# Other first rounds of attention, later rank products, low parts and row sums on TensorE in three slots, and held loads before the last stage

## The chip, the cores and the metric

The kernel runs on one core of a Trainium2 chip. Its five engines have instruction queues of their own: TensorE (PE; its weight loads are listed apart as PEld), VectorE (DVE), ScalarE (ACT), GpSimd (POOL) and SyncE (SP). SyncE does no arithmetic here: it issues transfers between the memory of the chip (DRAM) and the on-chip memory, and every transfer runs on the same 16 DMA engines, whoever issues it. The metric is the device time of one launch in microseconds.

## The reference

Three parts follow one another, all in float32:

```
scores = q @ k^T / 8 - log(448)            # 4 batches, 12 heads, 448 tokens, 64 wide
x  = (1 / (1 + exp(-scores))) @ v          # to (1792 tokens, 768)
logits = norm(x) @ norm(emb)^T / tau       # 8 experts, each token takes the largest
y  = softmax(logits)[e] * (relu(x @ w1[e]) @ w2[e])    # 768 -> 1024 -> 768
h  = y @ w_in                              # 768 -> 2048
g  = (a0 + a1 h + a2 h^2 + a3 h^3) / (1 + |b0| |h| + |b1| h^2 + 1e-6)
out = g @ w_out                            # 2048 -> 768
```

## The kernel before

Most products are made at float32 accuracy from a high and a low part: an operand is rounded to a short float32 form (`fp32r`), the rest is kept as a second such number, and three products are summed (high with high, high with low, low with high).

**Attention** (`attention`) goes over 12 double pairs of heads, called rounds `T`. In a round TensorE makes the scores of two pairs (`scores`, three chunks of 128 keys each; the last 64 keys of both pairs share one tile, `scores3`), ScalarE takes the sigmoid, TensorE multiplies the pair of the round before with v (`values`, `values3`) and transposes it (`transp`), and VectorE copies it out. `load` issues a pair's four key and query transfers, `load_v` those of v for a group of three pairs. The program order within a round is the order on every engine's queue. Beside it, in steps (`work`), VectorE decodes blocks of the 64-bit last-stage weights (`side_work`, `decode_steps`), for which `fetch` issues raw blocks of 768 KB on SyncE. Its route (`route_steps`, a generator of which 11 steps are taken per round) picks the expert of each token; its rank product (L298 to L314) counts, on TensorE, how many tokens before a token chose the same expert. Ahead of the first scores TensorE runs 21 products of zeros (L361) as fillers.

**Experts** (`experts`). `plan` deals the tokens into at most 21 slots of one expert each. Slots 14 to 20 are run under a condition, and each slot exists in two forms of which one is taken by a branch: a full one (128 tokens) and a small one (up to 64 tokens, whose high and low parts share one set of columns). VectorE prepares each expert's weights in four half-weights, high (L671) and low (L678), and signals `rdy`; it waits for `don` from ScalarE before it overwrites a weight. In a slot the hidden rows are transposed (in the small form folded, L756) into PSUM, ScalarE copies them out as high part and as raw, and GpSimd subtracts them to the low part (L761, L768). In the small form the two halves of the result rows are copied out by ScalarE and added by GpSimd (L815). GpSimd also issues the gather of the token rows (L706) and their scatter (L858). `less` makes a low part on TensorE: it subtracts the high part from what already lies in PSUM, by a product with the negative identity, and ScalarE copies the rest out.

**Last stage** (`ffn`). Weight blocks are loaded (`load`), split into high and low (`split`, ScalarE and VectorE) and written back to DRAM (`keep`) for the three later token groups. `rows` loads 512 token rows, in four parts for the first group, `gate` scales them on VectorE, `first_x` runs 26 fillers, transposes the rows with 24 transposes and lets ScalarE and VectorE split them. Then `l1` and `l2` (L1004 to L1008 and L1052 to L1054) fill TensorE until the end.

Of the kernel before, what the change touches and what calls it, by code (L numbers as in the profile page):

```python
# [20 lines left out]
P = 128  # L21
# [10 lines left out]
NSLOT = 21  # L32
NSURE = 14
NPAIR = H // 2
NDP = B * NPAIR // 2
# [33 lines left out]
def constants(tc, st):  # L69
    nc = tc.nc  # L70
    cst = st["cst"]
    ident = cst.tile([P, P], F32, name="ident")
    nc.gpsimd.memset(ident, 0.0)
    nc.gpsimd.affine_select(
        out=ident, in_=ident, pattern=[[-1, P]], compare_op=ALU.not_equal, fill=1.0, base=0, channel_multiplier=1
    )
    iden = st["iden"]
    nc.gpsimd.tensor_copy(iden[:, :, :P], ident.unsqueeze(1).broadcast_to([P, NPAIR, P]))
    st["ident"] = ident
    neg = st["neg"] = cst.tile([P, P], F32R, name="neg")  # L80
    nc.gpsimd.tensor_scalar(neg, ident, -1.0, None, op0=ALU.mult)
    fold = st["fold"] = cst.tile([P, P // 2], F32, name="fold")
    nc.gpsimd.tensor_add(fold, ident[:, 0::2], ident[:, 1::2])
    bias_s = cst.tile([P, 1], F32, name="bias_s")
    nc.gpsimd.memset(bias_s, -math.log(S))
    st["bias_s"] = bias_s
# [39 lines left out]
def attention(tc, st, qT, kT, v, emb, tau, w_in, w_out, pa, pb):  # L126
# [16 lines left out]
    with ExitStack() as ctx:  # L143
# [8 lines left out]
        def load(pi):  # L152
            b, p = divmod(pi, NPAIR)
            qr = ap.tile([P, S], F32, name="qr", bufs=4)
            kr = ap.tile([P, S], F32, name="kr", bufs=4)
            for r in range(2):
                nc.sync.dma_start(kr[r * D : r * D + D], kT[b, :, 2 * p + r, :S])
                nc.sync.dma_start(qr[r * D : r * D + D], qT[b, :, 2 * p + r, :])
            pair[pi] = dict(q=qr, k=kr)
# [71 lines left out]

        def transp(pi):
            b, p = divmod(pi, NPAIR)
# [3 lines left out]
            for g in range(2):  # L237
                pt = pav.tile([P, 2, PW], F32, name="po", tag="po")
                for c in range(2):
                    c0 = (2 * g + c) * CP  # L240
                    nc.tensor.matmul(pt[:CP, c], lhsT=xs[:, c0 : c0 + CP], rhs=st["iden"][:, p], start=True, stop=True)  # L241
                nc.vector.tensor_copy(xrt[b][:CP, 2 * g : 2 * g + 2, p], pt[:CP])  # L242
# [15 lines left out]
        def route_steps(b):  # L258
# [25 lines left out]
            if not tail:  # L284
# [5 lines left out]
                else:  # L290
                    nc.vector.tensor_copy(OHs[:CP, b], s4)
            yield
            yield
# [62 lines left out]
        nc.gpsimd.dma_start(tr, tau.partition_broadcast(NE))  # L356
        load_v(0, 0, 2)
        load_v(0, 2, 4)
        load_v(1)
        wp = pav.tile([P, 512], F32, name="po")  # L360
        for _ in range(21):  # L361
            nc.tensor.matmul(wp, lhsT=wz[:, :P], rhs=wz, start=True, stop=True)
# [74 lines left out]
        for T in range(NDP + 2):  # L437
            if T < NDP:
                scores(2 * T)
            if T == 0:  # L440
                router_weights()
                load(2)
                load(3)
                for n in range(3):
# [9 lines left out]
            if T < NDP:  # L454
                work(2)
                scores(2 * T + 1)
            if T == 0:
                scores3(0)
            if 1 <= T <= NDP:
                transp(2 * T - 2)  # L460
                transp(2 * T - 1)
            if T + 2 < NDP:
                load(2 * T + 4)
                load(2 * T + 5)
            if T + 1 < NDP:
                scores3(T + 1)
# [168 lines left out]
def experts(tc, st, w1, w2, w_in, w_out):  # L635
# [5 lines left out]
    with ExitStack() as ctx:  # L641
# [106 lines left out]
        def h_hi(s, b0):  # L748
            d = S_[s]
            bb = slice(b0, b0 + 4)  # L750
            if d["small"]:
# [8 lines left out]
                nc.scalar.activation(raw, pt[:, :, :n], AF.Relu)  # L760
                nc.gpsimd.tensor_sub(lo, raw, hi)  # L761
                return
            pt = turn(d["hs"], b0, 4)
            hi, lo = full(d["h"], bb, 0), full(d["h"], bb, 1)
            nc.scalar.copy(hi, pt)
            raw = mp.tile([P, 4, P], F32, name="raw")
            nc.scalar.copy(raw, pt)
            nc.gpsimd.tensor_sub(lo, raw, hi)  # L768

        def h_lo(s, b0):  # L770
            pass

# [30 lines left out]
        def rows_out(s, u):  # L803
# [5 lines left out]
            if d["small"]:  # L809
                n = P // 2  # L810
                yl = mp.tile([n, N2], F32, name="yl", bufs=1)
                nc.scalar.copy(yl, py[n:])
# [99 lines left out]
def ffn(tc, st, out):  # L912
# [9 lines left out]
    with ExitStack() as ctx:  # L922
# [3 lines left out]
        ppa = ctx.enter_context(tc.tile_pool(name="fpa", bufs=1, space=PSUM, reuse_waits="tile"))  # L926
        X, R, WI, WO, G, acc, KEPT = {}, {}, {}, {}, {}, {}, {}

        def load(i):
# [29 lines left out]
        def rows(q, parts):  # L959
# [4 lines left out]
            for c in range(0, w // P, n):  # L964
                nc.sync.dma_start(yq[:, c : c + n], src[:, c : c + n])
            X[q] = dict(y=yq, n=w, c=w // P)
# [18 lines left out]
        def first_x():  # L985
            d = X[0]
            d["h"], d["l"] = [fw.tile([P, KD, 512], F32R, name=n) for n in ("xh", "xl")]
            pts = [ppa.tile([P, 512], F32, name=f"acc{k}") for k in range(KD)]
            for _ in range(26):
                nc.tensor.matmul(pts[0], lhsT=st["ones"], rhs=st["wz"], start=True, stop=True)  # L990
            for c in range(4):
                for k in range(KD):
                    nc.tensor.transpose(pts[k][:, c * P : (c + 1) * P], d["y"][:, c, k * P : (k + 1) * P], ident)  # L993
# [68 lines left out]

        for i in range(4):
            load(i)
        split(0)
        split(1)
        rows(0, 4)
        keep(0)
        load(4)
        load(5)  # L1070
        for c in range(4):
            gate(0, c)
        first_x()
        for i in range(NU + LF):
# [62 lines left out]
```

## Time and profile before

| | |
|---|---|
| median of three runs | 1045.91 us (1044.01 to 1048.17) |
| the profiled execution | 1043.8 us, its span 1042.0 us |
| TensorE busy | 1006.0 us, 97% of the span |
| VectorE, ScalarE, GpSimd busy | 722.6, 507.1, 143.6 us |
| mean granted clock of TensorE | 0.984 |
| attention, experts, last stage | to about 185, to about 550, to 1042 us |

A row of the timeline gives start, duration, engine, line, operation, output from inputs, form and count; in brackets stands the idle time before it and what ended that. [...] Matmul ends are modelled, so the spacing of starts says more than a duration.

### The profile page before, as it was taken

How to read it: one execution, taken by the hardware profiler on the slowest of the kernel's cores; microseconds unless marked ns; L12 is line 12 of the kernel's file. 1: busy time of each engine (PE TensorE's matmuls, PEld its weight loads, DVE VectorE, ACT ScalarE, POOL GpSimd, SP SyncE). 2: the span in 40 equal slices, each digit the busy share in tenths (PEclk: the TensorE clock that was granted, in tenths of full speed). 3: DMA queues.
4: the chain of work that ended last, by engine and by line, in shares of the span. 5: the costliest groups of instructions: out<-in, count | busy, mean ns of one | idle time of the engine just before them, and what ended most of it. 6: DMA issues, size and time to landing. Idle time of an engine off the chain costs nothing. (4 is left out here: it accounts for less than half of the span.)

```text
span 1042.0 us, 14389 instructions
## 1 busy us (share of the span) xinstructions
PE 1006.0 (97%) x5256; PEld 794.5 (76%) x5256; DVE 722.6 (69%) x1031; ACT 507.1 (49%) x860; POOL 143.6 (14%) x141
## 2 busy tenths in 40 slices
PE   8999999798999999999996999999999999999998
PEld 3444444487899898898984888888888888888998
DVE  1545564899706897296994999966766667666676
ACT  4557565632232332333333776745455564445664
POOL 2000000153323342242451000000000000000000
PEclk8999999899999999999998999999999999999999
DMA  7977886686915869267878986677655576555892
GB/s 215 273 226 208 230 256 205 208 279 220 348 50 180 260 204 370 86 221 286 270 218 326 418 333 262 267 251 293 219 182 181 188 273 208 195 194 193 323 400 88
DMA packets 106668, 250.22 MB, mean 240 GB/s; under 512 B 11912, under 2 KB 63240, under 8 KB 106576
## 3 DMA queue, kind: packets, MB, share of 16 engines
q1 hardware_dynamic: 103504, 234.40, 65.7%
q0 software_dynamic: 3072, 14.58, 4.1%
q8 instruction: 59, 0.97, 0.4%
q14 instruction: 33, 0.27, 0.1%
HBM read 193.89 MB, written 55.06 MB: 239 GB/s over the span
## 5 line engine op out<-in xcount | busy, mean ns | idle before, releaser
L1052 PE MATMUL acc<-gh,wo 128*128 128x512 f32 (+1 forms) x384 | 139.3, 363 | 0.3 <-DVE gh L1038 0.3
L1054 PE MATMUL acc<-gl,wo 128*128 128x512 f32 (+1 forms) x384 | 139.4, 363 | 0.0
L1053 PE MATMUL acc<-gh,wo 128*128 128x512 f32 (+1 forms) x384 | 139.2, 363 | 0.0
L1004 PE MATMUL ph<-xh,wi 128*128 128x512 f32 (+1 forms) x384 | 137.8, 368 | 0.1
L1005 PE MATMUL ph<-xh,wi 128*128 128x512 f32 (+1 forms) x384 | 136.1, 363 | 0.0
L1016 ACT COPY h<-ph 128x512 f32<-128x512 f32 (+1 forms) x64 | 34.1, 533 | 158.0 <-PE ph L1008 158.0
L1023 DVE SCALAR_TENSOR_TENSOR sq<-sq,ab,ab 128x512 f32<-128x512 f32 (+1 forms) x64 | 43.8, 684 | 90.6 <-ACT ab L1020 90.5
L1008 PE MATMUL ph<-xl,wi 128*128 128x512 f32 (+1 forms) x384 | 87.2, 363 | 0.0
L1004 PEld LDWEIGHTS ph<-xh,wi 128*128 128x128 f32 x384 | 72.5, 189 | 12.0 <-ACT xh L995 1.3
L1052 PEld LDWEIGHTS acc<-gh,wo 128*128 128x128 f32 x384 | 72.5, 189 | 11.8 <-DVE gh L1038 0.6
L1054 PEld LDWEIGHTS acc<-gl,wo 128*128 128x128 f32 x384 | 72.5, 189 | 11.4 <-DVE gl L1039 0.2
L1053 PEld LDWEIGHTS acc<-gh,wo 128*128 128x128 f32 x384 | 72.5, 189 | 11.1
L1005 PEld LDWEIGHTS ph<-xh,wi 128*128 128x128 f32 x384 | 72.6, 189 | 10.7
L1008 PEld LDWEIGHTS ph<-xl,wi 128*128 128x128 f32 x384 | 66.7, 189 | 11.2
L186 ACT ACTIVATE A<-sc,bias_s 128x896 f32<-128x896 f32 x72 | 67.3, 1004 | 12.1 <-PE sc L182 12.0
L788 PE MATMUL py<-w2h,h 128*128 128x384 f32 x256 | 63.0, 345 | 5.3 <-DVEq L680 5.3
L671 DVE CAST w0h<-raw 128x1536 fp32r<-128x1536 f32 x14 | 12.8, 956 | 79.1 <-ACTq L801 77.1
L242 DVE COPY xr<-po 112x272 f32<-112x272 f32 x48 | 21.1, 442 | 62.0 <-PE po L241 61.5
L788 PE MATMUL ph<-w0h,x 128*128 128x512 f32 x192 | 58.2, 403 | 4.7 <-DVEq L680 2.2
L788 PE MATMUL py<-w3h,h 128*128 128x384 f32 x256 | 62.1, 342 | 0.0
L182 PE MATMUL sc<-qr,kr 64*128 64x448 f32 x288 | 61.9, 563 | 0.0
L798 ACT ACTIVATE hs<-ph 128x512 f32<-128x512 f32 x38 | 22.8, 599 | 77.8 <-PE ph L788 77.8
(210 smaller groups left out, 2062.0 us busy)
## 6 DMA issues: line engine op xcount, KB each, us to landing
raw<-in_w_dram SPq DMA_DIRECT2D x64, 768.0 KB, 6.3
wi<-ws SPq DMA_DIRECT2D x48, 768.0 KB, 4.3
wo<-ws SPq DMA_DIRECT2D x48, 768.0 KB, 5.8
raw<-in_w_in_dram SPq DMA_DIRECT2D x16, 768.0 KB, 6.2
raw<-in_w_out_dram SPq DMA_DIRECT2D x16, 768.0 KB, 6.9
wd<-dec SPq DMA_DIRECT2D x32, 384.0 KB, 7.8
rw<-wd SPq DMA_DIRECT2D x16, 768.0 KB, 6.7
ws<-wi SPq DMA_DIRECT2D x16, 768.0 KB, 6.3
```

Source lines behind the costliest of these rows:

```text
L182: nc.tensor.matmul(sc[:, r, :S], lhsT=d["k"][rs, c * P : (c + 1) * P], rhs=d["q"][rs], start=True, stop=True)
L186: nc.scalar.activation(A, sc[:, :, :S], AF.Sigmoid, bias=st["bias_s"], scale=0.125)
L788: m = nc.tensor.matmul(d[u], lhsT=a, rhs=w, start=(g == 0 and n == 0), stop=(g == 1 and n == len(work) - 1))
L798: nc.scalar.activation(d["hs"][:, u * 512 : u * 512 + 512], d.pop(u), AF.Copy if d["small"] else AF.Relu)
L1004: nc.tensor.matmul(ph, lhsT=w[:, 0, js], rhs=xh[:, k], start=(k == 0), stop=False)
L1005: nc.tensor.matmul(ph, lhsT=w[:, 1, js], rhs=xh[:, k], start=False, stop=False)
L1008: nc.tensor.matmul(ph, lhsT=w[:, 0, js], rhs=xl[:, k], start=False, stop=(k == KD - 1))
L1016: nc.scalar.copy(h, ph)
L1023: nc.vector.scalar_tensor_tensor(sq, sq, ab1, ab, op0=ALU.mult, op1=ALU.add)
L1052: nc.tensor.matmul(a, lhsT=w[:, 0, js], rhs=gh, start=(f == 0), stop=False)
L1053: nc.tensor.matmul(a, lhsT=w[:, 1, js], rhs=gh, start=False, stop=False)
L1054: nc.tensor.matmul(a, lhsT=w[:, 0, js], rhs=gl, start=False, stop=(f == NF - 1))
```

## The change

Four places, and some constants and memory layout that belong to them (`halves` sums the two halves of 128 partitions; `gap` and `G0` shift where the last stage's tiles lie).

- Start of attention: 12 fillers instead of 21; the query tiles of pairs 0 and 1 are issued by ScalarE; group 0 of v is issued whole, then pairs 2 and 3, and group 1 of v only after the router's weights; the fourth-chunk scores of round 1 move from round 0 into round 1.
- Routing: one more empty step ahead of the rank product, and the last pair's transposes take their PSUM tiles from the scores' pool.
- Slots 0 to 2 (`LEAD`): the hidden low parts by `less` on TensorE (in the small form after four products with the identity that bring the raw rows back into PSUM), the small form's row sum by two products with `halves`.
- Last stage: blocks 0 and 1 are loaded, then the rows, whose odd parts ScalarE issues; after the gates VectorE signals `there`, and SyncE waits for it before blocks 2 to 5 and the first write-back. Block 1 is split after the first token rows. 14 fillers in four lots stand between the transposes instead of 26 ahead of them.

```diff
-                nc.sync.dma_start(qr[r * D : r * D + D], qT[b, :, 2 * p + r, :])
+                (nc.scalar if pi < 2 else nc.sync).dma_start(qr[r * D : r * D + D], qT[b, :, 2 * p + r, :])
...
             yield
+            yield
             if tail:
...
-        load_v(0, 0, 2)
-        load_v(0, 2, 4)
-        load_v(1)
+        load_v(0)
+        load(2)
+        load(3)
         wp = pav.tile([P, 512], F32, name="po")
-        for _ in range(21):
+        for _ in range(12):
...
                 router_weights()
-                load(2)
-                load(3)
+                load_v(1)
...
-            if T == 0:
-                scores3(0)
+            if T < 2:
+                scores3(T)
             if 1 <= T <= NDP:
                 transp(2 * T - 2)
-                transp(2 * T - 1)
+                if T < NDP:
+                    transp(2 * T - 1)
+                else:
+                    transp(2 * T - 1, psc, "sc")
...
-            if T + 1 < NDP:
+            if 0 < T < NDP - 1:
                 scores3(T + 1)
...
-                nc.gpsimd.tensor_sub(lo, raw, hi)
+                if s < LEAD:
+                    d["hp", b0] = (raw, hi, lo)
+                else:
+                    nc.gpsimd.tensor_sub(lo, raw, hi)
                 return
             pt = turn(d["hs"], b0, 4)
             hi, lo = full(d["h"], bb, 0), full(d["h"], bb, 1)
             nc.scalar.copy(hi, pt)
+            if s < LEAD:
+                d["hp", b0] = (pt, hi, lo)
+                return
...
         def h_lo(s, b0):
-            pass
+            d = S_[s]
+            if s >= LEAD:
+                return
+            src, hi, lo = d.pop(("hp", b0))
+            if not d["small"]:
+                less(src, hi, lo)
+                return
+            pt = ppt.tile([P, 4, P], F32, name="pt")[:, :, : P // 2]
+            for c in range(4):
+                nc.tensor.matmul(
+                    pt[:, c], lhsT=ident, rhs=src[:, c], start=(c == 0), stop=False, skip_group_check=True
+                )
+            less(pt, hi, lo)
...
-                yl = mp.tile([n, N2], F32, name="yl", bufs=1)
+                yl = mp.tile([P, N2], F32, name="yl", bufs=2)
+                if s < LEAD:
+                    nc.scalar.copy(yl, py)
+                    nc.scalar.sem_inc(don[u], 1)
+                    d["yl", u] = yl
+                    for v in (2, 3) if u == 3 else ():
+                        pt = ppt.tile([P, 4, P], F32, name="pt")[:n].rearrange("p c n -> p (c n)")[:, :N2]
+                        nc.tensor.matmul(pt, lhsT=st["halves"], rhs=d.pop(("yl", v)), start=True, stop=True)
+                        nc.scalar.copy(d["ys"][:n, (v - 2) * N2 : (v - 1) * N2], pt)
+                    return
...
+        there = tc.alloc_semaphore("there")
+        fp.tile([P, 8], F32, name="gap", bufs=1)
+        G0 = [fp.tile([P, 512], F32R, name="gh", bufs=3)]
...
-                nc.sync.dma_start(yq[:, c : c + n], src[:, c : c + n])
+                eng = nc.scalar if parts > 1 and c % 2 else nc.sync
+                eng.dma_start(yq[:, c : c + n], src[:, c : c + n])
...
-            for _ in range(26):
-                nc.tensor.matmul(pts[0], lhsT=st["ones"], rhs=st["wz"], start=True, stop=True)
+            wp = pph.tile([P, 512], F32, name="ph")
             for c in range(4):
+                for _ in range(3 if c else 5):
+                    nc.tensor.matmul(wp, lhsT=st["ones"], rhs=st["wz"], start=True, stop=True)
                 for k in range(KD):
...
-        for i in range(4):
-            load(i)
+        load(0)
+        load(1)
+        rows(0, 4)
         split(0)
+        for c in range(4):
+            gate(0, c)
+        nc.vector.sem_inc(there, 1)
+        nc.sync.wait_ge(there, 1)
+        first_x()
         split(1)
-        rows(0, 4)
+        load(2)
+        load(3)
         keep(0)
         load(4)
         load(5)
-        for c in range(4):
-            gate(0, c)
-        first_x()
```

## Rows read from the trace of the kernel before

**Rows 1.** Busy time per stretch: engines with counts, granted clock, DMA share, GB/s.
```profile
0.00:25.00 25.00, 20.89 (x81) 7.80 (x83) 3.45 (x8) 11.36 (x14) 6.34 (x23) 0.88 0.70 208
...
20.00:22.50 2.50, 2.50 (x10) 0.55 (x6) 0.00 (x0) 0.95 (x1) 0.00 (x0) 0.50 1.07 364
...
230.00:260.00 30.00, 26.09 (x119) 22.74 (x118) 28.99 (x23) 7.80 (x16) 11.05 (x8) 0.89 0.71 241
...
430.00:431.00 1.00, 0.00 (x0) 0.00 (x0) 0.00 (x0) 0.42 (x1) 0.30 (x1) 1.00 0.00 0
...
547.00:548.00 1.00, 1.00 (x8) 1.00 (x7) 0.00 (x0) 0.00 (x0) 0.00 (x0) 1.00 1.06 442
```

**Rows 2.** Waits of TensorE: for whom, us in total, times, longest.
```profile
PE rk L298 <- DVE OHb L283: 1.2, 2, 0.6
PE rk L298 <- DVE s L286: 0.8, 1, 0.8
...
PE py L788 <- DVEq L680: 3.5, 2, 1.8
PE ph L788 <- DVEq L680: 2.2, 1, 2.2
...
PE acc L990 <- PEq L907: 8.7, 1, 8.7
```

**Rows 3.** Timeline of TensorE, rounds 0 and 1 of attention.
```profile
1.26 6.61 PE L362 MATMUL po<-wz 128*128 128x512 bf16 x21 [1.26 <-DVE wz L351]
7.80 2.53 PE L182 MATMUL sc<-qr,kr 64*128 64x448 f32 x12
...
16.69 1.45 PE L195 MATMUL sc<-qr,kr 64*64 64x448 f32 x4 [2.53 <-DMA qr<-in_qT_dram]
...
26.71 4.73 PE L222 MATMUL po<-A,vt 128*64 128x448 f32 x24
...
33.83 2.43 PE L241 MATMUL po<-iden,xs 128*112 128x136 f32 x16
36.19 0.98 PE L195 MATMUL sc<-qr,kr 64*64 64x448 f32 x8
```

**Rows 4.** Timeline of ScalarE and SyncE in the same rounds.
```profile
8.96 5.66 ACT L186 ACTIVATE A<-sc,bias_s 128x896 f32<-128x896 f32 x6 [2.39 <-PE sc L182]
...
17.64 0.59 SPq L397 DMA_DIRECT2D raw<-in_w_in_dram  x1
...
31.15 0.47 SPq L158 DMA_DIRECT2D qr<-in_qT_dram  x1
```

**Rows 5.** Timeline of TensorE, slot 0 (small form).
```profile
205.35 1.00 PE L756 MATMUL pt<-fold,hs 128*128 128x64 f32 x8
```

**Rows 6.** Groups by form, VectorE, 205 to 260 us: count, busy, mean ns, idle before.
```profile
L678 DVE TENSOR_TENSOR w2l<-raw,w2h 128x1536 fp32r<-128x1536 f32 x4 | 8.3, 2087 | 0.0
...
L678 DVE TENSOR_TENSOR w1l<-raw,w1h 128x1536 fp32r<-128x1536 f32 x4 | 6.8, 1746 | 0.0
L671 DVE CAST w2h<-raw 128x1536 fp32r<-128x1536 f32 x4 | 5.5, 1386 | 0.7 <-issue 0.4
...
L671 DVE CAST w3h<-raw 128x1536 fp32r<-128x1536 f32 x4 | 3.8, 948 | 0.0
```

**Rows 7.** Branches by line (ns min/median/max, first and last start).
```profile
L907 PEldq COMPARE_BRANCH  x1: 5522/5522/5522, 546.7 to 546.7; - x1
...
L868 PEldq COMPARE_BRANCH  x1: 3247/3247/3247, 427.8 to 427.8; - x1
```

**Rows 8.** Timeline of TensorE and VectorE, start of the last stage.
```profile
558.02 7.48 PE L990 MATMUL acc<-wz,ones 128*128 128x512 bf16 x26 [8.71 <-PEq L907]
565.31 0.62 DVE L973 TENSOR_SCALAR yq<-yq,gr 128x768 f32<-128x768 f32 x1 [0.35 <-DMA yq<-yd]
565.34 2.78 PE L993 MATMUL acc<-ident,yq 128*128 128x128 f32 x24
```

**Rows 9.** The page's transfers: count, KB each, median us from issue to landing.
```profile
rw<-wd SPq DMA_DIRECT2D x16, 768.0 KB, 6.7
```

More of the change, by code (lines that the diff above doesn't have):

```diff
@@ L33 @@
 NSURE = 14
+LEAD = 3
 NPAIR = H // 2
@@ L83, in constants @@
     nc.gpsimd.tensor_add(fold, ident[:, 0::2], ident[:, 1::2])
+    halves = st["halves"] = cst.tile([P, P // 2], F32, name="halves")
+    nc.gpsimd.tensor_add(halves, ident[:, : P // 2], ident[:, P // 2 :])
     bias_s = cst.tile([P, 1], F32, name="bias_s")
@@ L230, in values, with transp @@
             nc.scalar.copy(xs, po[:, :S])
-        def transp(pi):
+        def transp(pi, pool=pav, tag="po"):
             b, p = divmod(pi, NPAIR)
@@ L237, in transp @@
             for g in range(2):
-                pt = pav.tile([P, 2, PW], F32, name="po", tag="po")
+                pt = pool.tile([P, 2, PW], F32, name=tag, tag=tag)
                 for c in range(2):
@@ L810, in rows_out @@
                 n = P // 2
-                yl = mp.tile([n, N2], F32, name="yl", bufs=1)
+                yl = mp.tile([P, N2], F32, name="yl", bufs=2)
[8 more added lines that the diff above has]
+                    return
+                yl = yl[:n]
                 nc.scalar.copy(yl, py[n:])
```

## The prediction, made before the result was known

> **What bounds the kernel now.** I read the stretches first: TensorE is busy nearly everywhere, so time is only to be won where it stands still, runs at half clock, or does work that is not needed. Two places stand out in [rows 1]: the first 25 us, with 20.89 us busy at a mean clock of 0.88, and 230 to 260 us, with 26.09 of 30 at 0.89. The waits of TensorE [rows 2] name the rest: 0.8 and 1.2 us in attention for the routing's vector chain, 3.5 and 2.2 us in the first expert slots for the weights that VectorE prepares, and 8.7 us before the last stage. After that TensorE hardly waits, so the last stage's products only shift with their start. The change touches exactly these places; I price them one by one.
>
> **1. Start of attention.** Before, TensorE ran 21 filler products until 7.87, the scores of pairs 0 and 1, and then stood: the key and query tiles of pairs 2 and 3 came late (wait of 2.53 us ending at 16.69, [rows 3]), after which the clock was at 0.50 [rows 1], its lower level. The fourth-chunk scores of round 1 started at 36.19 [rows 3]. Three chains can set that moment in the new order.
> - TensorE and ScalarE. Twelve fillers: the 21 took 6.61 us, and 12 of them at full clock would be 2.6, so nine fewer end about 2 us sooner: about 5.75. The four tiles of pair 0 leave by 2.0 on two queues instead of 3.2 on one; they did not hold the scores up at 7.80, and I assume that they don't at 5.75. The six sigmoids cost 5.66 us [rows 4] and begin about 1.7 us sooner than 8.96, at 7.2, as ScalarE first has to issue four transfers and load a table; then 0.94 for the last chunk: 13.8. The fourth-chunk scores of round 1 no longer stand ahead of the values of round 0, so the late tiles stop nothing there. Fourth-chunk values 0.9 (as many products as the scores that took 0.98), scores 2.5, values 4.7, scores 2.5, the moved fourth-chunk scores 0.9, transposes 2.4 [rows 3]: 27.6, and 29.3 if a hole of 1.6 us before 13.8 lowers the clock as it did before.
> - Transfers. SyncE issues 18 transfers of 0.6 us ahead of the first raw block, where it was 24 and a stall: 12.2 where it was 17.64 [rows 4]. The last query tile of pairs 4 and 5 left at 31.15 [rows 4], held by the raw blocks ahead of it. Moved by the same 5.4 us it leaves at 25.8 and, as it stands behind four blocks of 768 KB, lands near 29. By bytes: six pairs (2.7 MB), two groups of v (1.3) and four raw blocks (3.1) make 7.2 MB.
> - VectorE has ten decode steps ahead of the first transposes' copies. They begin when the first raw block lands, which moves with its issue; its copies then come about when the transposes need them.
> I take 29.1, so 7.1 us of gain. Bounds: 8.6 if TensorE alone sets it, 4.5 if the transfers only keep a mean of 244 GB/s. The tiles moved behind (group 1 of v, the raw blocks) are first needed about 20 us or later; their cover is this same stretch.
>
> **2. Rank products.** One more empty step puts the rank product of batches 0 to 2 into the next round, where its one-hot rows have long been written. The waits of 0.8 and 1.2 us [rows 2] go: 2.0 us. The rest of the steps still fit into the 11 of the next round, so nothing is late there. Bounds 1.2 and 2.1. The last pair's transposes get score banks and need not wait for two copies: 0.2.
>
> **3. Slots 0 to 2.** Slots 0 and 1 take the small form (folded products appear in them), slot 2 the full one. What goes: GpSimd's subtractions and row sums, during which VectorE is slower: four casts of the one half-weight took 5.5 us and four of the other 3.8, four differences 8.3 and 6.8 [rows 6], work of one size. The disturbed ones lie beside a GpSimd instruction; about two thirds of those go, the rest are indirect transfers and stay: some 2 us for each of the two experts prepared here. What comes, on TensorE: in a small slot each of two low parts takes four products against the identity, priced as the four folds (1.00 us busy at 205.35 [rows 5], so 0.9 pipelined), and one product of 256 columns (0.3, an estimate from these): 2.4. The second low part is needed at once, so TensorE waits for ScalarE's copy: 0.65, an estimate from 0.94 us for 896 columns [rows 4] and the hand-overs. The row sums are two products of 384 columns; twelve such calls of 448 columns, two at a time, took 4.73 [rows 3], so 0.67 each, and 0.2 of waiting: 1.5. Together 4.5 a small slot, 9.0 for two, and 0.6 in slot 2: 9.6 us more TensorE work and waiting.
> Against it stand the waits of 3.5 and 2.2 us [rows 2], which VectorE no longer causes once TensorE is later by 4 us and VectorE sooner by 2, and the stretch at half clock that follows them: 0.11 of 30 us [rows 1], 3.3. That is 9.0, or some 9.9 with smaller hand-overs. I enter 0: VectorE's late weights turn into TensorE work of the same length. Bounds: 2.0 slower (waits stay in part) and 3.5 faster (low parts hidden, as ScalarE's copies already are).
>
> **4. Start of the last stage.** TensorE's wait of 8.7 us [rows 2] is the jump over two unused slots: two branches, the longer 5.52 us [rows 7], while the transfer engines are full (share 1.06 at 547) with four loads of 768 KB. A branch of 3.25 us was paid where transfers were idle (0.00 at 430, [rows 1, 7]). Two of the four loads now come later, so the second branch, some 5.1 us, should fall into an empty stretch: 1.9 us less. [...]
> After release it took 7.3 us to the gating of the fourth row block (565.31) and 10.1 to the end of 24 transposes [rows 8]. Now the four row loads leave on two queues, without two spills and two loads behind them, and one pair of weight subtractions fewer stands ahead of the gates: first gate done at about +5.0, last at +7.0. TensorE then has 24 transposes (2.78) and nine fillers in between (0.22 each at full clock): +9.8. [...] I take the middle, 10.7: 0.6 lost of the 1.9, 1.3 us gained. What is late next: splitting block 1 and block 2 now stands between the row tiles and the first activation on ScalarE; block 2's load is issued near 562 and has to land in 8 us, against a median of 6.7 [rows 9]. Bounds: 4 faster, 1 slower.
>
> **Sum.** 7.1 + 2.0 + 0.2 + 0 + 1.3 = 10.6 us. The profiled execution took 1043.8 us (span 1042.0 and 1.8 around it): 1033.2. The median of the three runs is 2.1 us above it, so I predict 1035.3.
>
> **Rivals.**
> - The lead is given back to transfers. If the first 7.2 MB move at the 208 GB/s of the first 25 us [rows 1], they take 34.6 us, and round 1 gains 1.5 instead of 7.1: 1041. For it: transfers are the late chain in part 1. Against it: that mean contains the start and a hole, and between 20 and 22.5 us 364 GB/s were reached [rows 1]. 0.16.
> - More than forecast: VectorE, freed of GpSimd, lets the slots gain 3, and both branches shrink to 3.3 with the row loads sooner, 2 to 3 us more: 1029.5. For it: the branch of 3.25. Against it: the first branch still runs beside two loads. 0.14.
> - Slower: the clock in slots 0 to 2. The new waits for ScalarE (0.65 and 0.2 in each small slot) break TensorE's stream where it was closed. If the clock then sits at half, every 1 us of products at full clock takes 2. Slots 0 to 2 lie between about 201 and 259 us and hold nearly 50 us of products; from 11 us of them at half clock on, the whole gain is eaten, and with a third, some 15 us, it is 1050. For it: after waits of 1.8 and 2.2 us the clock fell [rows 1, 2]. Against it: around the waits of 0.8 and 0.6 us in attention [rows 2] the rounds kept their length. [...] 0.05.
>
> **Chances and range.** The forecast with its own spread, 1031 to 1039.5, has 0.62; the rivals 0.16, 0.14 and 0.05, and 0.03 is left for things not seen. Half a per cent, 5.2 us, is what a measurement of this kernel can tell from no change: 1040.7. Faster: 0.62, 0.14 and half of 0.16, so 0.84; same 0.10; slower 0.06. The range for 8 in 10 is 1029 to 1041: it takes in most of the second rival and the near half of the first.
>
> **What would show it.** Part 1: fillers end near 5.75, the first raw block is issued near 12, fourth-chunk scores of pairs 4 and 5 begin near 29, the clock stays at 1.00 or falls once. Part 2: no wait of the rank product on VectorE. Part 3: no GpSimd subtraction in slots 0 to 2, no wait for VectorE's weights, slot 3 starting as long after slot 0 as before (58 us); a shorter or longer span there shows my zero wrong. Part 4: a branch of 3.3 us, row gates done some 7 us after release, the first product of the last stage 1 to 2 us sooner in its own frame; an idle TensorE after the first three blocks would show the held loads too late. The prediction is wrong if round 2 of attention starts after 34 us or if slot 3 starts over 3 us off.

## The result, and the profile after

The changed kernel takes 1053.15 us (median of 8 runs, 1051.87 to 1056.94) against 1045.87 of the kernel before in the same session (8 runs, 1040.66 to 1048.17): ratio 1.0073, 95% interval 1.0058 to 1.0088. It is slower by 0.7%, where 1035.3 us was forecast, 1% faster. Its profiled execution took 1052.9 us with a span of 1051.2, so the two traces are 9.1 us apart.

The page after: span, busy time, the queue that brings instructions, and the costliest group.
```profile
span 1051.2 us, 14424 instructions
...
PE 1014.2 (96%) x5281; PEld 798.2 (76%) x5281; DVE 717.3 (68%) x1031; ACT 508.8 (48%) x864; POOL 123.0 (12%) x132
...
q8 instruction: 59, 0.97, 0.4%
...
L1091 PE MATMUL acc<-gh,wo 128*128 128x512 f32 (+1 forms) x384 | 141.1, 367 | 0.4 <-DVE gh L1077 0.4
```

The same stretches as in [rows 1], columns as there.
```profile
0.00:25.00 25.00, 22.08 (x102) 8.63 (x104) 5.91 (x11) 14.36 (x18) 6.44 (x24) 0.93 0.86 254
20.00:22.50 2.50, 2.50 (x16) 0.92 (x14) 1.92 (x3) 0.67 (x2) 0.00 (x0) 1.00 0.98 302
230.00:260.00 30.00, 29.37 (x146) 25.01 (x146) 29.07 (x32) 8.73 (x19) 4.56 (x5) 1.00 0.79 271
430.00:431.00 1.00, 0.97 (x10) 0.73 (x7) 1.00 (x1) 0.95 (x2) 0.56 (x1) 1.00 0.00 0
```
The places that [rows 1] marked are better: the granted clock is 1.00 where it was 0.50 and 0.89, TensorE works 29.37 of 30 us at 230, and it no longer stands still at 430. In both traces the granted clock is either 1.00, TensorE at full speed, or 0.50; a figure between is a mean over a stretch. The 26 fillers of [rows 8] started 0.427 us apart at 0.50 (to 561.4 us) and 0.216 at 1.00 (from 561.7 on). The loss must lie where nothing was looked for. TensorE's waits, against [rows 2], name the first part of it:
```profile
PE ph L812 <- issue: 8.4, 4, 3.9
PE ph L1030 <- PEq L941: 7.5, 1, 7.5
PE acc L1032 <- DVE yq L1011: 2.9, 1, 2.9
...
PE py L812 <- DVEq L686: 1.2, 1, 1.2
PE py L812 <- ACT h L738: 0.9, 2, 0.5
...
PE po L244 <- DVE xr L245: 0.6, 1, 0.6
```
The rank product's waits are gone and those for VectorE's weights fell from 3.5 and 2.2 to 1.2; but 8.4 us in front of an expert's first products are put down to nothing ("issue"). The branches show why. First the kernel before, all jumps of the line of [rows 7] (ns min/median/max), then the changed kernel, where L902 answers to L868 and L941 to L907:
```profile
L868 PEldq COMPARE_BRANCH  x35: 68/281/3247, 199.7 to 546.4; - x35
...
L902 PEldq COMPARE_BRANCH  x35: 68/281/4807, 192.5 to 548.5; - x35
L941 PEldq COMPARE_BRANCH  x7: 67/68/6139, 454.8 to 555.2; - x7
```
Followed from one marker to the next (us; the first product of slots 0, 3 and 18 and of the last stage's first block, and the end):

| stretch | before | after | difference | forecast |
|---|---|---|---|---|
| to slot 0 | 201.07 | 193.82 | -7.25 | -9.3 |
| slots 0 to 2 | 58.07 | 58.61 | +0.54 | 0 |
| slots 3 to 17 | 273.44 | 282.74 | +9.30 | 0 |
| slot 18 to the last stage | 35.68 | 35.86 | +0.18 | -1.3 |
| last stage's products | 473.77 | 480.12 | +6.35 | 0 |

The two large terms stand in code that the diff doesn't touch or only moves in memory. In slots 3 to 17 the jumps into the half-filled form of slots 15 and 17 took 4807 ns (at 473.9 us) and 3996 ns (at 512.8), where before they took 234 and 229; the one of slot 12 fell from 3247 to 230. Behind each slow one TensorE's granted clock was 0.50, behind the second from 517.1 to 523.8 us, and here behind the first (stretch, TensorE's busy time, granted clock, DMA share, GB/s):
```profile
479.50:482.90 3.40, 3.13 (x8) 0.50 0.00 0
```
In the last stage the products of its first layer (`ph`) start 0.2276 us (before) and 0.2284 us (after) apart on average, hardly different, but those of its second layer (`acc<-gh`, `acc<-gl`, "second products" below) 0.2267 before and 0.2334 after; 864 of them have full width, and 6.7 ns for each make 5.8 of the 6.35 us. It is not the clock: from 600 to 1000 us it is granted at 1.00 in both kernels.

### The profile page after: what moved, and what is told of

It reads as the page before. It is cut to its first block, busy times and chain, and to the rows that moved or that the text cites. A ratio compares the mean times of both kernels' runs of the same rounds, so it can differ in the third digit from the quotient of the medians.

```text
span 1051.2 us, 14424 instructions
## 1 busy us (share of the span) xinstructions
PE 1014.2 (96%) x5281; PEld 798.2 (76%) x5281; DVE 717.3 (68%) x1031; ACT 508.8 (48%) x864; POOL 123.0 (12%) x132
## 5 line engine op out<-in xcount | busy, mean ns | idle before, releaser
L1091 PE MATMUL acc<-gh,wo 128*128 128x512 f32 (+1 forms) x384 | 141.1, 367 | 0.4 <-DVE gh L1077 0.4
L1092 PE MATMUL acc<-gh,wo 128*128 128x512 f32 (+1 forms) x384 | 140.3, 365 | 0.0
L812 PE MATMUL ph<-w1h,x 128*128 128x512 f32 x192 | 60.6, 403 | 0.0
```

The lines of the kernel that those rows point to most:

```text
L812: m = nc.tensor.matmul(d[u], lhsT=a, rhs=w, start=(g == 0 and n == 0), stop=(g == 1 and n == len(work) - 1))
L1091: nc.tensor.matmul(a, lhsT=w[:, 0, js], rhs=gh, start=(f == 0), stop=False)
L1092: nc.tensor.matmul(a, lhsT=w[:, 1, js], rhs=gh, start=False, stop=False)
```

## Experiments: slots 3 to 17

First theory: what decides is where a jump and its target stand in TensorE's list of instructions. The rival: the transfers at that moment. A count of places is used below, made in the programs, as the traces have none: every instruction of TensorE's list, run or not, is one. A product is two (a load of weights and a multiply), an F32 product four (two of both, as the traces count them: the four folds of [rows 5] are x8). Never-run code moves all that follows:
```diff
+PAD = {2: 12}                # x1, x2; x3: {13: 60}
...
+            more = PAD.get(s, 0) if d["small"] and (u, g) == (0, 0) else 0
+            work = work[:1] * more + work
...
-                    d[u], lhsT=a, rhs=w, start=(g == 0 and n == 0), ...
+                    d[u], lhsT=a, rhs=w, start=(g == 0 and n <= more), ...
```

**x1.** 

> The changed kernel, with 12 products added in front of slot 2's half-filled form. Slot 2 takes its full form with this data, so the added products are never run; they only move all code behind them by 24 places in TensorE's list of instructions. Theory (the place of a jump in the instruction list decides whether its target is already there): the jumps of slots 15 and 17, 4807 and 3996 ns in the changed kernel, fall to about 0.25 us, the half clock behind them goes too, slots 14 to 17 lose the 11 us that they had gained, and the time is about 1042 against 1053.2. Rival (the jumps are slow because of what the transfers do at that moment): both stay at 4 to 5 us and the time stays at 1053. The last stage's second products stay at 0.2335 us spacing under both.

Measured: 1053.21 us (ratio to before 1.0086, 1.0063 to 1.011). The jumps kept 4942 and 3892 ns. The theory in this form failed, or the step was too small.

**x2.** 

> The kernel before, with the same 12 never-run products in slot 2's half-filled form. Theory of the place: the jump of 3247 ns at 427.8 us falls to about 0.25 us, no other becomes slow, and the kernel gains 2 to 3 us: 1043 to 1044 against 1045.9. Rival (transfers): the jump stays, 1045.9.

Measured: 1053.91 us (1.0086, 1.006 to 1.0113): 9 us slower by twelve products that never run. That transfers alone do it is out; my guess of which places are good was wrong. The slow jump stayed (3332 ns), and slots 15 and 17 stall, though their jumps took 228 and 223 ns: slot 15 behind its first product, slot 17 in front of it:
```profile
484.17 0.40 PE L791 MATMUL ph<-w0h,x 128*128 128x512 f32 x1
487.12 0.50 PE L791 MATMUL ph<-w0l,x 128*128 128x512 f32 x1 [2.55 <-issue]
...
524.04 0.50 PE L791 MATMUL ph<-w0h,x 128*128 128x512 f32 x1 [1.86 <-issue]
```

**x3.** 

> The kernel before, with 60 never-run products in slot 13's half-filled form (slot 13 takes the full one). That puts the jumps of slots 15 and 17 at the very places that they have in the changed kernel, and leaves the jump at 427.8 us where it was. Theory of the place: these two jumps become 4 to 5 us long, TensorE runs at half clock for a time behind them, and the kernel loses 10 to 11 us: 1056. Rival (transfers, or the changed start of the slots): no jump changes, 1045.9.

Measured: 1057.1 us (1.0111, 1.0081 to 1.0141). Both jumps became slow, 3501 and 4066 ns, with nothing of the change in the kernel. One more jump did that I had not expected, the one over the 60 added products (4203 ns):
```profile
L871 PEldq COMPARE_BRANCH  x35: 67/281/4203, 197.2 to 560.6; - x35
```

**What fits all of it.** Instructions come in packets of 0.97 MB / 59 = 16.4 KB (q8 above). How many fill one shows where TensorE's code runs straight on: from 584.9 to 990.7 us of the kernel before 1910 products and 1909 loads of weights were recorded, and 15 packets were moved, 255 instructions for each (the stretch, with columns as in [rows 1], and the queue in it):
```profile
584.90:990.70 405.80, 405.80 (x1910) 339.68 (x1909) 304.39 (x470) 228.47 (x372) 0.00 (x0) 1.00 0.67 244
q8 instruction: 15, 0.25, 0.2%
```
I take blocks of 256 places, an estimate from these 255; y1 below, 296 places longer, took 60 packets. The two stalls of x2 lie right behind places 8144 and 8912 of the list, three times 256 apart: there, I take it, a block begins. A full expert ends with a jump over its half-filled form, and 1 us later the next slot's jump over its full form follows, some 385 places on in all. Counted from the start of the block in which the first of the two stands:

| kernel, slot | from | to | jump, ns |
|---|---|---|---|
| before, 12 | 229 | 611 | 3247 |
| before, 15 and 17 | 96, 100 | 483, 487 | 234, 229 |
| after, 12 | 93 | 475 | 230 |
| after, 15 and 17 | 216, 220 | 603, 607 | 4807, 3996 |
| x1, 15 and 17 | 239, 243 | 626, 630 | 4942, 3892 |
| x2, 12 | 253 | 635 | 3332 |
| x2, 15 and 17 | 120, 124 | 507, 511 | 228, 223, then a stall |
| x3, 13 (one jump) | 223 | 513 | 4203 |

Of these all that go past 512, the end of the next block, are slow (3.2 to 4.9 us), and none that stays below is (0.22 to 0.23 us). I read this so: what lies past the end of the next block has not come yet when the jump wants it ("theory of the blocks" below). The queue agrees: the traces of the kernel before and the changed kernel have seven jumps of over 3 us; in each of them one packet of this queue started, and the jump ended 2.3 to 3.0 us after that start. This is the line for the jump into slot 15 of the changed kernel (473.9 to 478.7 us, the packet's start at 476.2):
```profile
q8 instruction: 1, 0.02, 1.5%
```
What sets the moment of a packet no run shows. Kernels with other places test the reading; y1 also is the base for the parts of the change:
```diff
+PAD = {2: 48, 13: 60}        # y1, y4; y2: {13: 48}; y3: {2: 56, 13: 60}
+PADF = {18: 40}              # the same in front of slot 18's full form
```

**y1.** By the count of places only the second jump over unused slots, 540 places on from the start of its block, passes the end of the next block here. 

> The kernel before with never-run products only: 48 in slot 2's and 60 in slot 13's half-filled form, 40 in slot 18's full form; these forms aren't taken with this data. [...] So the jump of 3247 ns falls to about 0.25 us, the first jump over unused slots (5522 ns) to about 0.4, the second becomes about 6.4, and the kernel gains 2 + 3.7 us: 1039 against 1045. Rival (the shifted code moved something else than the jumps, as transfers): slow jumps stay as many as before or turn up elsewhere, 1045 or slower.

Measured: 1042.23 us (0.9968, 0.9949 to 0.9986). The jumps into slots 12, 15 and 17 took 0.3 to 1.1 us, slots 3 to 17 lasted 271.70 in place of 273.44. The first jump over unused slots stayed slow, 6472 ns, against the expectation. It starts 61 places behind its block's start, and four others that start 51 to 63 places behind it took 0.7 to 1.4 us: the next block, I read this, had not landed yet. In y4 the same jump at the same place took 0.42 us, in y2 and y3 about 6. The queue shows the difference: from 538 to 544 us, ahead of this jump (544.0 in y1, 544.1 in y4), y4 moved a packet and y1 none; y1's came while the jump waited, from 544 to 550.5. First y4's line, then y1's:
```profile
q8 instruction: 1, 0.02, 1.8%
...
q8 instruction: 1, 0.02, 0.9%
```
Why it came so late in y1 stays open. z2 puts these jumps later in their blocks.

**z2** (the decode edit is read in the next section).
```diff
+PAD = {2: 26, 13: 66}
+PADF = {0: 40, 18: 50}
...
-                work(2)                               # rounds 0 and 1
+                work(2 if T != 1 else 0)              # twice, ahead of the transposes
...
+                work({0: 0, 2: 5, 3: 5}.get(T, 2))    # at the end of a round
```


> The attention part alone on the kernel before, as in y3, with two more edits. First, six decode steps of VectorE (two at the end of round 0 and four of round 1) are moved behind the first transposes and made up for in rounds 2 and 3. Theory of the attention part: TensorE's wait of 2.98 us at 30.03 and the half clock behind it come from VectorE, which does ten decode steps from 21.70 to 29.5 ahead of the copies that free the transposes' banks; with four steps ahead of them the wait goes and slot 0 starts at 191 to 193 instead of 195.8. Rival (transfers hold TensorE there anyway): 195 or later. Second, other never-run products: 40 in slot 0's and 50 in slot 18's full form, 26 in slot 2's and 66 in slot 13's half-filled form, so that the jump into an expert's half-filled form and the first jump over unused slots come 88 to 112 places behind the start of a block and not 56 to 68. Theory of the blocks: the next block has then landed; no slot's jump is over 0.45 us (0.9 to 1.6 in y3), and of the two jumps over unused slots only the second stays slow. Both together: 1028 to 1032 against 1037.5.

Measured: 1038.84 us (0.9946, 0.9924 to 0.9968). The placing did what was expected: none of 35 jumps at the experts is over 0.4 us, and of the seven others only the last is slow.
```profile
L875 PEldq COMPARE_BRANCH  x35: 68/225/397, 196.8 to 540.0; - x35
L914 PEldq COMPARE_BRANCH  x7: 68/68/6410, 457.5 to 543.2; - x7
```

## Experiments: the last stage's products

**x4.** The tile `gap` moves gh, gl and the other small tiles behind it by 32 bytes.
```diff
-        fp.tile([P, 8], F32, name="gap", bufs=1)
```


> The changed kernel without the 32-byte tile called gap at the start of the last stage, so that the tiles behind it, gh and gl among them, start 32 bytes lower; the early allocation of gh stays. Theory (the second products of the last stage are slower because of the starting byte of gh and gl): their spacing falls from 0.2335 back to 0.227 us and the stage gets 6.3 us shorter: 1046.8 against 1053.2. Rival (the shift by 256 bytes that the new tile halves brings, or the new place of gh among the tiles): the spacing stays at 0.2335 us, 1053. The jumps of slots 15 and 17 stay slow under both.

Measured: 1047.78 us (1.0037, 1.0017 to 1.0057), 5.4 less than the changed kernel and than x1; spacing 0.2267 us. Groups by form, 600 to 1000 us, of the kernel before, the changed kernel and then x4:
```profile
L1052 PE MATMUL acc<-gh,wo 128*128 128x512 f32 x272 | 105.8, 389 | 0.0
```
```profile
L1091 PE MATMUL acc<-gh,wo 128*128 128x512 f32 x276 | 109.3, 396 | 0.0
L1093 PE MATMUL acc<-gl,wo 128*128 128x512 f32 x276 | 109.1, 395 | 0.0
```
```profile
L1092 PE MATMUL acc<-gl,wo 128*128 128x512 f32 x274 | 106.7, 389 | 0.0
L1090 PE MATMUL acc<-gh,wo 128*128 128x512 f32 x273 | 106.2, 389 | 0.0
```
**z1.** `gap` with 16 columns in place of 8. 

> The changed kernel with a gap tile of 64 bytes instead of 32; gh, gl and the other tiles behind it then start at 32 bytes past a multiple of 64 again, as in the kernel before, but at other addresses than there. Theory (what counts for the second products is where gh and gl start within 64 bytes): spacing 0.227 us, the time as without the gap, 1047.8. Rival (any tile in front of them slows them down, or it is the distance between them and other tiles): spacing 0.2335 us, 1053.

Measured: 1051.31 us (1.0071, 1.0047 to 1.0095), spacing 0.2299, between the two that were expected. The start within 64 bytes alone isn't it.

**g1, g2, g3** put the shift into the kernel before.
```diff
+        fp.tile([P, 8], F32, name="gap", bufs=1)          # g1, g3: ahead of yq
...
+                fp.tile([P, 8], F32, name="gap2", bufs=1)  # g2; g3: 24 columns; ahead of gh
             gh = fp.tile([P, 512], F32R, name="gh", bufs=3)[:, :w]
```


> The kernel before with a gap tile of 32 bytes ahead of all small tiles of the last stage (yq, h, sq, ab, t1, n, gh, gl, ot), which then start 32 bytes higher; order of the tiles and jumps as in the kernel before. If the gap alone makes the second products slow: spacing 0.2334 us and 1051.5 against 1045.9. If it takes the early gh with it: 0.2267 and 1045.9.

> The same gap put right in front of gh, so that gh, gl and ot alone start 32 bytes higher. If the place of the operand that TensorE reads counts: spacing 0.2334 us, 1051.5. If the place of the tiles that ScalarE and VectorE work on counts (h, sq, ab, t1, n): 0.2267, 1045.9.

> The gap of 32 bytes at the front and another of 96 in front of gh, so that yq, h, sq, ab, t1 and n start 32 bytes higher and gh, gl and ot 128 bytes higher. If the place of gh and gl within 128 bytes counts: spacing 0.2267 us, 1045.9. If the place of the tiles that the other engines work on counts: 0.2334, 1051.5.

Measured: 1050.99 us (1.0066, 1.0038 to 1.0093), 1051.8 (1.0077, 1.005 to 1.0103) and 1051.18 (1.0063, 1.0041 to 1.0085); spacing 0.2334, 0.2334 and 0.2331. The first of the second products in g1:
```profile
L1054 PE MATMUL acc<-gh,wo 128*128 128x512 f32 x270 | 106.9, 396 | 0.0
```
32 bytes alone cost the kernel before 6 us, without the early gh. But moving gh and gl alone does it (g2), and so does moving the tiles that the other engines work on while gh and gl keep their place within 128 bytes (g3). Each theory is refuted by the other's kernel. What the fast kernels share is that all tiles of this stage, the weights too, start at the same place within 128 bytes (byte 32); whether that is the rule, and why it slows these products and hardly the first ones, stays open.

## Experiments: attention and the start of the last stage

**y3.** The hunks of attention and rank products alone, placed like y1. 

> The kernel before with the attention and rank product parts of the change alone, placed like the kernel before with never-run products (56 in slot 2, 60 in slot 13, 40 in slot 18). If these parts are worth what the trace of the changed kernel shows at slot 0, it is 7.2 us faster than the kernel before so placed: 1032. If the shorter time at slot 0 is given back in the slots (weights that come too late), 1035 to 1039.

Measured: 1037.54 us (0.9926, 0.9897 to 0.9954), 4.7 below y1. Slot 0 starts at 195.81 (y1: 200.41), and nothing is given back behind it: slots 0 to 2 last 58.01. So the 193.82 of the changed kernel was an early execution. Over the seven profiles with this attention the start has the median 196.03, over the eight with the old one 199.88; the gain is 3.9 us, of which I put 2.0 down to the rank waits. TensorE and VectorE in y3:
```profile
25.87 1.18 PE L243 MATMUL po<-iden,xs 128*112 128x136 f32 x8
30.03 1.58 PE L243 MATMUL po<-iden,xs 128*112 128x136 f32 x8 [2.98 <-DVE xr L244]
```
```profile
21.70 0.56 DVE L527 TENSOR_SCALAR dec<-raw 128x768 int32<-128x768 int32 x1 [11.86 <-DMA raw<-in_w_in_dram]
...
28.66 0.96 DVE L536 SCALAR_TENSOR_TENSOR dec<-dg,dec 128x768 f32<-128x768 f32 x1
29.54 0.78 DVE L244 COPY xr<-po 112x272 f32<-112x272 f32 x2
```
```profile
30.00:35.00 5.00, 4.97 (x26) 2.78 (x26) 4.04 (x7) 0.60 (x1) 0.00 (x0) 0.66 0.75 220
```
The copies that free the transposes' banks stand behind ten decode steps, and those begin only when the first raw block has landed, at 21.7. TensorE now comes for the second half of the transposes nearly 3 us before them, and behind this wait the granted clock is low again, 0.66 from 30 to 35 us.

z2 took six of the ten steps away from there. The transposes run through (16 in one group from 26.08), but then TensorE waits 1.02 us for a query tile, and the steps made up for later delay rounds 3 and 4 (by 0.58 and 3.13 us): slot 0 starts at 198.16, and the total of 1038.84 misses the 1028 to 1032 expected. Both theories were half right: VectorE held TensorE first, a transfer did so next.
```profile
29.53 2.39 PE L197 MATMUL sc<-qr,kr 64*64 64x448 f32 x7 [1.02 <-DMA qr<-in_qT_dram]
```
```profile
PE po L243 <- DVE xr L244: 3.7, 2, 3.1
```

**y2.** The changed kernel without `gap`, with PAD and PADF as above. 

> The changed kernel without the gap tile, with never-run products: 48 in slot 13's half-filled form and 40 in slot 18's full form. Theory of the blocks: the jumps of slots 15 and 17 and the first jump over unused slots are fast; with the gap gone the change is left with what its parts do, -7.2 in attention and rank products, +0.5 in slots 0 to 2, 0 at the start of the last stage, against the kernel before placed in the same way: 1032 to 1033. Rival (the code of later slots isn't the cause): 1047.8 as without the gap alone.

Measured: 1038.72 us (0.9936, 0.9914 to 0.9957). That is 9.1 below x4 (measured in another session) by the place of the code alone; in the traces slots 3 to 17 last 270.97 us in place of 280.53. And it is 3.5 below y1: what the parts of the change are worth together when code and tiles lie well. It is no better than y3 with its fewer parts.

**y4.** The last stage's hunks alone, without `gap` and `G0`, on y1. 

> The kernel before with the last stage's part of the change alone (held loads, row loads on two queues, gates and first transposes ahead of the second block, fewer fillers), without the gap tile and the early allocation of gh, placed as the kernel before with never-run products. If the prediction's step was right, it is 1.3 us faster than the kernel before so placed; by the trace of the changed kernel it is equal within 0.5 us: 1039.

Measured: 1042.96 us (0.9986, 0.9966 to 1.0005), equal to y1. TensorE (L998 fillers, L1000 transposes) and VectorE's last gate:
```profile
558.66 1.51 PE L1000 MATMUL acc<-ident,yq 128*128 128x128 f32 x6 [2.85 <-DVE yq L979]
559.82 1.15 DVE L979 TENSOR_SCALAR yq<-yq,gr 128x768 f32<-128x768 f32 x2 [0.72 <-DMA yq<-yd]
559.97 1.49 PE L998 MATMUL ph<-wz,ones 128*128 128x512 bf16 x3
561.25 1.49 PE L1000 MATMUL acc<-ident,yq 128*128 128x128 f32 x6
562.53 1.49 PE L998 MATMUL ph<-wz,ones 128*128 128x512 bf16 x3
563.81 1.12 PE L1000 MATMUL acc<-ident,yq 128*128 128x128 f32 x6
564.77 0.81 PE L998 MATMUL ph<-wz,ones 128*128 128x512 bf16 x3
565.42 0.82 PE L1000 MATMUL acc<-ident,yq 128*128 128x128 f32 x6
```
All rows are gated at 560.97, 7.8 us after the second jump's end (553.2), but the transposes end at 566.2: after the idle 2.85 us the granted clock is 0.50 until 564, three fillers take 1.49 us in place of 0.65, and they stand between the blocks. Against y1 the second jump ends 4.0 us sooner (553.2 for 557.2), but the first product comes only 1.3 us sooner (566.4 for 567.7).

**z3.** z2 and y4 together, with the fillers up front.
```diff
-                for _ in range(3 if c else 5):
+                for _ in range(0 if c else 16):
```


> As z2, with the last stage's part of the change (no gap, no early gh), but 16 filler products ahead of the first transposes and none between them. Theory of that part: the transposes came late because TensorE ran nine fillers and 18 transposes at half clock, some 1.5 us for each three and each six, while the gated rows were there; without fillers in between, the first product of the last stage comes 33 to 34 us after slot 18's start instead of 36.1 as in y4, and the kernel is 2 us faster than z2: 1027 to 1029. Rival (row loads set that moment): equal to z2.


```profile
551.49 6.43 PE L1001 MATMUL ph<-wz,ones 128*128 128x512 bf16 x16 [5.70 <-PEq L914]
557.76 1.47 PE L1003 MATMUL acc<-ident,yq 128*128 128x128 f32 x12
559.75 1.53 PE L1003 MATMUL acc<-ident,yq 128*128 128x128 f32 x12 [0.53 <-DVE yq L982]
561.41 0.50 PE L1014 MATMUL ph<-xh,wi 128*128 128x512 f32 x1
```
Measured: 1039.07 us (0.9953, 0.9935 to 0.9971), equal to z2, not 2 us faster. The stage's start did as expected: the granted clock is back at 1.00 from 557.7, when the transposes begin, and the first product comes 32.25 us after slot 18's start (z2: 34.77, y4: 36.14). In this execution slot 0 started 2.1 us and slot 3 3.0 us later than in z2, and the products after the start took 0.8 longer.

**b1.** y3's attention, z3's last stage and placing, slots 0 to 2 as before. 

> The kernel before with the attention part as the change has it (decode steps where they were), the last stage's part with 16 fillers ahead of the first transposes and none between, no gap, no early gh, no edit of slots 0 to 2, and the never-run products of z2 and z3. From the traces: slot 0 at 195.8 as in y3; 328.2 to 329.0 from there to slot 18 as in z2 and z3 (all jumps into experts fast); 32.3 from there to the last stage's first product as in z3; 474.8 from there to the end: a span of 1031 to 1032, some 1033 in time, against 1045 of the kernel before and 1037.5 of y3. If z3's time was no better than z2's because the last stage's part costs again what it saves, 1037 as y3.

Measured: 1034.87 us (0.9899, 0.9866 to 0.9931), faster than both kernels, and some 2 us above the expected 1033. In its profiled execution (1036.56 us) slot 0 started at 198.28 in place of 195.8; the other stretches came within 0.5 us of the expected.

## Why the prediction was wrong

- **The steps that failed most had no term in the sum.** "After that TensorE hardly waits, so the last stage's products only shift with their start" holds for waits, not for the products' own length: +6.35, of which `gap` makes 5.4 (x4; g1 shows it in the kernel before); some 0.8 stay without it (474.58 in x4), unexplained. `gap` and `G0` stand in the diff, and I gave them no line.
- **Slots 3 to 17 were taken as unchanged.** The forecast read 3247 and 5522 ns of [rows 7] as the price of a jump in a given transfer load. That there are 229 and 3247 ns for the same kind of jump in one trace should have been the question. Added and removed TensorE instructions ahead of them moved two jumps past the end of the next block and one back before it: +9.3 by the traces. x3 makes the same jumps slow in the kernel before; y2 gets 9.1 back by place alone.
- **Attention start, -7.1.** The step that failed is "its copies then come about when the transposes need them". I had put the first raw block's issue at 12.2; it was 13.56 (changed kernel) and 14.38 (y3), and it landed 7 us later. The first scores began at 5.81 (5.75 forecast) and the fourth-chunk scores of round 2 began at 29.95 (29.1) in the changed kernel, but at 31.54 in y3. By the medians the start is worth 1.9 at slot 0 (3.9 less the 2.0 of the rank products), below my bound of 4.5.
- **Rank products, -2.0.** Right: no such wait is left. The 0.2 of the last transposes could not be told apart.
- **Slots 0 to 2, 0.** Right within its bounds: +0.54, and 58.6 to 58.9 in all profiles with this part but 58.0 to 58.1 in nearly all without it. The granted clock stayed at 1.00 from 194 to 252.4 us in spite of the new waits for ScalarE (0.9 us in all), so the slower rival was not what happened. The zero was a balance of some 9 us on either side, which no run measured apart.
- **Start of the last stage, -1.3.** The second jump fell from 5.12 to 3.42 us, by 1.7 of the 1.9 forecast, but the first rose from 5.52 to 6.14, and the loads alone do not set their price: the first took 0.43 us in x2 with the loads as before, the second 6.1 in y4 with the held ones. The gates came 7.4 us after the first filler (7.0 forecast), but behind its idle time TensorE ran fillers and transposes at 0.50: the last transposes ended 12.0 us after the first filler and not 10.7. The step that failed is the half clock, of which I had taken only half. The 10.7 lies midway between 9.8 and 11.7, with 1.9 more for a low clock; that term rests on a full rate of TensorE that no run shows. What the trace of the kernel before showed in its place: at the spacing of 0.216 us that they have at a granted clock of 1.00, the 26 fillers of [rows 8] would take 5.6 us (an estimate from it), and they took 7.48, again 1.9 more. A jump's own price was 67 to 88 ns in these runs where it isn't taken, 170 to some 430 ns where it is and doesn't stall, and 3.1 to 6.7 us where it stalls.

The parts that I did price come to some -3.5 (y2 against y1) in place of -10.6. The two times differ by 7.3 us, the two traces by 9.1; runs of one kernel spread over 5 to 9 us, much of it already there at slot 0 (197.1 to 201.1 in eight profiles of the old attention), so terms below 1 us rest on one stretch of one trace each. By the prediction's own signs of being wrong nothing had shown: round 2 began at 29.95, not after 34, and slot 3 started 2.6 us off, not over 3. Both look only at what lies ahead of slot 3.

## What to carry to other kernels

Before trusting a sum of edits, look for what the diff moves without touching: code behind an inserted instruction, and tiles behind an inserted tile. A branch that costs 0.2 us in one place and 4 us in another was here a question of where the target lies, and never-run code is a cheap test for it. Fillers that are to bring up TensorE's clock served here in front of the awaited work (z3, granted clock 1.00 from the first transpose on), not between its pieces (y4, 0.50 until 564 us).

## What the runs showed of the hardware

- Twelve products that never run made the kernel 9 us slower (x2), others 4 us faster (y1).
- TensorE's instructions come in packets of 16.4 KB, one for 255 recorded instructions in straight code, and the jumps fit blocks of 256 places each. A jump past the end of the next block (two within 1 us counted from the first) cost 3.1 to 6.7 us; one into the next block 0.2 to 0.4 when the jump stood 82 or more places behind its block's start (0.9 once, in y4), and up to 1.6 at 34 to 69.
- The first jump over unused slots stands within that reach, but early in its block, in nine kernels. At place 21 (kernel before, g1 to g3) or 60 to 61 (y1 to y3) it took 5.5 to 6.9 us in seven, at 45 and 61 (x2, y4) 0.43 and 0.42. In y1 and y4 the next packet came behind the jump's start where it was slow and ahead of it where it was fast; what sets that moment is open. The second such jump, right behind the first, was slow in every kernel (2.8 to 6.4 us).
- 32 bytes of shift of some tiles of the last stage lengthen the spacing of its second products from 0.2267 to 0.2334 us, 3%, with no wait in the profile and the granted clock at 1.00.
